# Sink scores behind two scores of their group, and the first expert's weights in halves around v rows

## The chip, the cores and the metric

The kernel runs on one core of a Trainium2 chip. Its time is the device time of one execution in microseconds; a kernel is given by the median of its runs. The engines are TensorE (PE, with its weight loads as PEld), VectorE (DVE), ScalarE (ACT), GpSimd (POOL) and SyncE (SP). POOL and SP also issue the DMA transfers.

## The reference

Attention over a window of 128 keys and four sink keys feeds a mixture of four experts. The sizes are: batch 4, 8 heads, 768 tokens, head dimension 64; 3072 tokens in all for the experts, with model width 512 and hidden width 1024.

```python
scores = scale * np.matmul(q, k.transpose(0, 1, 3, 2))
keep = is_sink | in_window               # 4 sinks, 0 <= i - j < 128
scores = np.where(keep, scores, -1e9)
a = np.exp(scores - max); a = a / (sum(a) + 1e-9)
x = matmul(a, v) as [3072, 512]          # heads side by side
p = domain_probs / (domain_probs.sum(-1, keepdims=True) + 1e-9)
for e in range(4):
    out += p[:, e:e+1] * (relu(x @ w1[e]) @ w2[e])
```

## The kernel before

A batch of attention (`Attention(b)`) is cut into three groups of 256 tokens and four pairs of heads. For each group and pair the steps are: turning of the q and k rows on TensorE (`transposes`, L499, the "flips", into `tr`), a copy of the turned block to `qkT` by ACT or DVE (L222), the window scores (`scores`, L601, `sps`), the exponential on ACT (L626, `aT`), a mask on DVE (L635 in the first batch), the values (`values`, L660 and L667, `od`), the division on DVE (L694, L697, `onat`) and a turn of the result to `xT` (`turn`, L725). In the third and fourth batch the q and k rows are turned by DMA transposes on SP instead (`turn_nat`, L198).

From the second group on, the scores with the four sink keys are a step of their own (`sinks`, L566): four products into one bank, for all four head pairs, and one exponential to `sinkA` (L574). They need the turned q rows of all four pairs of the group and the sink keys `ksd`, which POOL forms for the first batch (L529). The values of the group need `sinkA`.

The expert part (`Mixture`) makes hidden blocks H from `xT` and w1 (L958 and L1035, `hps` and `cps`), gated on DVE with rows that SP loads (`load_gate`, L385), and the output from H and w2 (L1245 for the first batch, L1175 for the others). From the second batch on it uses fewer products, with sums formed on DVE.

A planner written in the kernel sets the order of all engines. It keeps a clock for each engine in the table `t`, with one for the software DMA queue (`t["sw"]`) and one for the hardware DMA queue (`t["hw"]`). It books each step with a fixed cost, and at each turn emits the step that can start soonest by these clocks. Six PSUM banks go round (`pick`, `take`). Within a batch, the steps of keys, sinks and scores come in the order of the list `todo`. Where no step can start within 220 ns of the planner's clock, it puts in a product of zeros (`idle_products`, L481). Loads are issued on POOL in the order of a list, the first of them by the lines that stand ahead of the planner's loop. `lands` books the arrival of a load, and a step that needs it isn't planned ahead of that time. A changed booking or a changed place in `todo` therefore can give another order for all that comes after.

The list for a batch before the change:

```python
for g in range(NG):
    if g == (1 if b == 0 else 0):
        self.todo.append(("keys", b, 0, 0))
    if g:
        self.todo.append(("sinks", b, g, 0))
    self.todo += [("scores", b, hp, g) for hp in range(NHP)]
```

Of the kernel before, what the change touches and what calls it, by code (L numbers as in the profile page):

```python
# [12 lines left out]
BF16 = mybir.dt.bfloat16  # L13
# [3 lines left out]
def kernel(  # L17
# [17 lines left out]
    E, Dm, F = moe_w1.shape  # L35
    Ntok, Dout = out.shape

    P = 128
# [7 lines left out]
    NHP = H // 2  # L46
    NDB = Dm // P
# [23 lines left out]
    t = {"pe": 1200.0, "act": 0.0, "dve": 0.0, "pool": 1280.0, "sp": 800.0, "sw": 6500.0, "hw": 0.0}  # L71
# [81 lines left out]
    landed = {}  # L153
    ROW = {64: 12.8, 128: 22.6, 512: 79.8, 1024: 156.2}

    def lands(key, rows, cols, *deps):
        issued = pool(0, *deps, fixed=880)
        t["sw"] = max(t["sw"], issued + 1500) + rows * ROW[cols] / 16
        landed[key] = t["sw"] + 900
# [8 lines left out]
    wpool = ctx.enter_context(tc.tile_pool(name="wpool", bufs=1))  # L168
# [14 lines left out]
    def load_nat(b, tb):  # L183
        both = sb.tile([P, 2, H, D], BF16, name="qkn", tag="qkn", bufs=NQB)
        for i, src in enumerate((q, k)):
            nc.gpsimd.dma_start(  # L186
                out=both[:, i], in_=src[b, :, tb * P:(tb + 1) * P, :].rearrange("h p d -> p h d"),
            )
            lands(("qk", b, tb), H * P, D, qkn_free[0])
        qkn_free.pop(0)  # L190
        qkn_free.append(1e12)
        nat[b, tb] = both
# [56 lines left out]
    def load_v(b, ts):  # L249
        for tb in ts:  # L250
            nc.gpsimd.dma_start(  # L251
                out=vx[tb][:, :, 0:D],
                in_=v[b, :, tb * P:(tb + 1) * P, :].rearrange("h p d -> p h d"),
            )
            lands(("v", b, tb), H * P, D, values_at[b - 1, min(NG - 1, (tb + 1) // 2)] if b else 0.0)

    w1_sb, w2_sb = {}, {}

    def load_w1(e, parts=1):
        w1_sb[e] = wpool.tile([P, NDB, F], BF16, name=f"w1_{e}", tag=f"w1_{e}")  # L260
        n = F // parts
        for i in range(parts):
            nc.gpsimd.dma_start(
                out=w1_sb[e][:, :, i * n:(i + 1) * n],
                in_=moe_w1[e][:, i * n:(i + 1) * n].rearrange("(db p) f -> p db f", p=P),
            )
            lands(("w1", e, i), Dm, n)
            landed["w1", e] = landed["w1", e, i]

    def load_w2(e):  # L270
        w2_sb[e] = wpool.tile([P, NFB, Dout], BF16, name=f"w2_{e}", tag=f"w2_{e}")
        nc.gpsimd.dma_start(out=w2_sb[e], in_=moe_w2[e].rearrange("(fb p) d -> p fb d", p=P))
        lands(("w2", e), F, Dout)
# [147 lines left out]
    t["sw"] += 500  # L421
    for tb in (2, 3):
        load_nat(0, tb)
    load_v(0, (2, 3))
    load_w1(0, 2)
    t["sw"] += 200
    load_w2(0)

    nc.vector.tensor_copy(out=ident, in_=identf)
# [311 lines left out]
    class Attention:  # L741


        def __init__(self, b):
            self.b = b
            self.flips = [("transposes", b, g, hp) for g in range(NG) for hp in range(NHP)] if b < 2 else []
            self.todo, self.scored, self.valued = [], [], []
            for g in range(NG):
                if g == (1 if b == 0 else 0):
                    self.todo.append(("keys", b, 0, 0))  # L750
                if g:
                    self.todo.append(("sinks", b, g, 0))
                self.todo += [("scores", b, hp, g) for hp in range(NHP)]
            self.total = len(self.todo) + len(self.flips) + (1 if b else 2) * NG * NHP
            self.steps = 0

# [525 lines left out]
    for e in (1, 2):  # L1282
        loads += [(load_w1, e), (load_w2, e)]
# [19 lines left out]
    while mix.more() or att.more():  # L1303
        now = t["pe"]

        if not att.more() and not loaded:
            loaded = 1
            gates_by_row()
            loads += [(load_w1, 3), (load_w2, 3)]
            for tb in range(NQB):  # L1310
                loads.append((load_nat, 1, tb))
                if tb % 2:
                    loads += [(load_v, 1, (tb - 1,)), (load_v, 1, (tb,))]
# [88 lines left out]
```

The softmax here doesn't subtract the row's maximum and nothing guards it: scores larger than these inputs give would overflow.

## Time and profile before

| | |
|---|---|
| median of 5 runs | 379.82 us (379.02 to 381.03) |
| the profiled execution | 379.02 us |
| its span, first to last instruction | 377.3 us |
| TensorE busy | 368.7 us, 3966 products |
| VectorE busy | 270.3 us |
| ScalarE busy | 147.7 us |
| software DMA queue (POOL's) | 17.31 MB, 51.4% of the span of 16 engines |
| hardware DMA queue (SP's and others) | 17.18 MB, 20.8% |

The span is what the profile sees; the time of the execution has a little around it. A busy share is the union of the instructions' times. As products of TensorE overlap in its pipeline, the distance between their starts tells more than their durations. A timeline row gives the start and the length of a series of like instructions in microseconds, the engine, the line and the operation, what is written and read, the shape and the count, and in brackets the idle time ahead of the series with what ended it.

### The profile page before, as it was taken

The page shows a single profiled execution, that of the slowest core. Times are in us where ns is not written, and L with a number is a line of the kernel's source. Part 1 is how long each engine was busy: PE and PEld are TensorE (multiplying, and loading weights), DVE is VectorE, ACT ScalarE, POOL GpSimd, SP SyncE. Part 2 cuts the span into 40 slices and gives each one's busy share as a digit, 9 for nine tenths or more (in the row PEclk, how much of TensorE's full clock was granted, in tenths as well). Part 3 has the DMA queues.
Part 4 walks back from the last instruction along what each step waited for, and adds up shares of the span by engine and source line. Part 5 has one row for each costly group of instructions (what it writes and reads, how often), then busy time and mean ns, then how long its engine had stood idle before and what let it go on. Part 6 is the DMA issues. An engine that isn't in the chain of part 4 may idle for free.

```text
span 377.3 us, 9471 instructions
## 1 busy us (share of the span) xinstructions
PE 368.7 (98%) x3966; PEld 299.6 (79%) x3966; DVE 270.3 (72%) x610; ACT 147.7 (39%) x386; POOL 71.1 (19%) x91
## 2 busy tenths in 40 slices
PE   7999999999999999999998999999999999999995
PEld 3676767566667788888887888889999999999984
DVE  5665987765346997785697499489589496795780
ACT  4856434766455255436415446452112011111110
POOL 8945114702812091010200000000000000000000
PEclk9999999999999999999999999999999999999999
DMA  9999999951999999234394421122021111210101
GB/s 165 176 173 201 210 210 175 155 49 7 144 197 162 198 134 128 71 43 59 70 179 103 57 57 30 30 80 63 0 85 30 55 33 28 71 30 2 57 3 56
DMA packets 110807, 35.61 MB, mean 94 GB/s; under 512 B 94260, under 2 KB 106132, under 8 KB 110764
## 3 DMA queue, kind: packets, MB, share of 16 engines
q0 software_dynamic: 77520, 17.31, 51.4%
q1 hardware_dynamic: 32188, 17.18, 20.8%
q8 instruction: 31, 0.51, 0.6%
q10 hardware_dynamic: 1056, 0.52, 0.5%
q14 instruction: 12, 0.10, 0.1%
HBM read 40.45 MB, written 6.34 MB: 124 GB/s over the span
## 4 chain that ended last, share of the span: by engine, by line
PE 89%; DVE 5%; ACT 2%; DMA 2%; issue 1%; ACTq 0%; DVEq 0%
PE hps L958 28%; PE acc L1175 28%; PE acc L1245 11%; PE cps L1035 11%; PE sps L601 4%; PE od L667 3%; DMA kraw<-in_k_dram 1%; DVE H L982 1%; PE tr L499 1%; ACT onat L706 1%; PE od L660 1%; DMA gates<-gate_rows 1%; DVE H L1054 1%; PE acc L481 1%; PE sinks L566 1%
## 5 line engine op out<-in xcount | busy, mean ns | idle before, releaser
L958 PE MATMUL hps<-xT,w 128*128 128x256 bf16 x1056 | 131.7, 273 | 0.4 <-ACT aT L626 0.2
L958 PEld LDWEIGHTS <-w 128*128 128x128 bf16 x1056 | 99.3, 98 | 14.7 <-issue 2.3
L1175 PEld LDWEIGHTS <-H 128*128 128x128 bf16 x720 | 67.9, 98 | 11.2 <-issue 3.7
L626 ACT ACTIVATE aT<-sps 128x512 bf16<-128x512 f32 (+1 forms) x96 | 47.9, 572 | 34.2 <-PE sps L601 34.2
L982 DVE SCALAR_TENSOR_TENSOR H<-hps,gates 128x512 bf16<-128x512 f32 x84 | 57.3, 686 | 4.7 <-PE hps L958 3.6
L1175 PE MATMUL acc<-w,H 128*128 128x256 bf16 x432 | 56.4, 273 | 0.4 <-ACT acc L1199 0.4
L706 ACT ACTIVATE onat<-od,R 128x64 bf16<-128x64 f32 x144 | 33.2, 323 | 44.5 <-DVE R L694 44.4
L1245 PE MATMUL acc<-w,H 128*128 128x512 bf16 x192 | 45.4, 379 | 0.0
L251 POOL DMA_DIRECT2D vx<-in_v_dram x24 | 21.3, 896 | 80.9 <-PE od L667 70.9
L1175 PE MATMUL acc<-wf,H 128*128 128x256 bf16 x288 | 35.4, 273 | 0.8 <-ACT osb L1208 0.8
L1208 ACT COPY osb<-acc 128x256 f32<-128x256 f32 x36 | 13.5, 374 | 54.9 <-PE acc L1175 54.4
L620 DVE TENSOR_TENSOR aT<-aT,mask 128x1024 bf16<-128x1024 bf16 (+1 forms) x36 | 22.9, 641 | 14.0 <-ACT aT L626 13.9
L1245 PEld LDWEIGHTS <-H 128*128 128x128 bf16 x192 | 18.0, 98 | 18.1 <-issue 0.8
L1035 PEld LDWEIGHTS <-w 128*128 128x128 bf16 x480 | 30.6, 98 | 1.7 <-issue 0.8
L1054 DVE SCALAR_TENSOR_TENSOR H<-cps,gates 128x512 bf16<-128x512 f32 x45 | 30.7, 683 | 0.1
L1175 PEld LDWEIGHTS <-S 128*128 128x128 bf16 x288 | 27.7, 98 | 3.5 <-issue 0.3
L971 ACT ACTIVATE H<-hps 128x512 bf16<-128x512 f32 x35 | 21.1, 605 | 22.3 <-PE hps L958 22.3
L1063 ACT COPY cps<-cps 128x512 f32<-128x512 f32 x15 | 8.7, 582 | 44.1 <-PE cps L1035 44.1
L1035 PEld LDWEIGHTS <-vf 128*128 128x128 bf16 x360 | 22.5, 98 | 0.7 <-issue 0.2
L186 POOL DMA_DIRECT2D qkn<-in_k_dram x22 | 20.1, 913 | 9.8 <-DMA w<-in_moe_w_dram 8.5
L186 POOL DMA_DIRECT2D qkn<-in_q_dram x22 | 20.0, 908 | 8.9 <-DMA w<-in_moe_w_dram 3.9
L1257 DVE SCALAR_TENSOR_TENSOR osb<-acc,scale_t,osb 128x512 f32<-128x512 f32 x18 | 13.5, 749 | 9.4 <-PE acc L1245 9.3
(96 smaller groups left out, 435.8 us busy)
## 6 DMA issues: line engine op xcount, KB each, us to landing
w<-in_moe_w_dram POOLq DMA_DIRECT2D x7, 1024.0 KB, 19.3
out_dram<-osb SPq DMA_DIRECT2D x24, 256.0 KB
gates<-gate_rows SPq DMA_DIRECT2D x36, 128.0 KB
vx<-in_v_dram POOLq DMA_DIRECT2D x24, 128.0 KB, 6.4
qkn<-in_q_dram POOLq DMA_DIRECT2D x22, 128.0 KB, 7.3
qkn<-in_k_dram POOLq DMA_DIRECT2D x22, 128.0 KB, 7.3
w<-in_moe_w_dram POOLq DMA_DIRECT2D x2, 512.0 KB, 7.8
kraw<-in_k_dram ACTq DMA_DIRECT2D x2, 256.0 KB
```

Of the source, the lines that this page charges most:

```text
L186: nc.gpsimd.dma_start(out=both[:, i], in_=src[b, :, tb * P:(tb + 1) * P, :].rearrange("h p d -> p h d"),)
L251: nc.gpsimd.dma_start(out=vx[tb][:, :, 0:D], in_=v[b, :, tb * P:(tb + 1) * P, :].rearrange("h p d -> p h d"),)
L620: nc.vector.tensor_mul(a, a, m[:, None, :].to_broadcast([P, 2, w]))
L626: nc.scalar.activation(out=a[:, ph], in_=sps[ph][:, 0:w], func=AF.Exp, scale=scale)
L706: nc.scalar.mul(o[:, qi, hp, ph * D:(ph + 1) * D], od[:, qi, ph, 0:D], R[:, qi, ph])
L958: nc.tensor.matmul(h[:, i].rearrange("p (q n) -> p q n", q=2), lhsT=w1_sb[e][:, db, fb * P:(fb + 1) * P], rhs=xT[b, g][:, :, db], start=(i ...
L971: nc.scalar.activation(out=dst, in_=h, func=AF.Relu)
L982: nc.vector.scalar_tensor_tensor(out=dst, in0=h, scalar=0.0, in1=gate, op0=ALU.max, op1=ALU.mult,)
L1035: nc.tensor.matmul(y[:, f], lhsT=A[:, d, f * P:(f + 1) * P], rhs=T[:, d], start=(m in ("P1", "P5") and f == 0 and d == 0), stop=(d == 1), ...
L1054: nc.vector.scalar_tensor_tensor(out=dst, in0=src, scalar=0.0, in1=gate, op0=ALU.max, op1=ALU.mult)
L1175: nc.tensor.matmul(x, lhsT=self.operand(b, g, e, m)[:, f], rhs=forms[e][m][:, f], start=(k == 0 and f == 0 and m in ("P1", "P5")), stop=(k ...
L1245: nc.tensor.matmul(op, lhsT=H[:, fb // QF, fb % QF, s], rhs=w2_sb[e][:, fb, :], start=(fb == 0), stop=(fb == NFB - 1),)
```

## The change

It has two parts. The sinks of the first batch now stand in `todo` behind the first two scores of their group, instead of ahead of all four (`insert(2 - NHP, ...)`, that is, two from the end); in the other batches their place stays the same. And of the two halves of expert 0's w1 the first is now issued ahead of the v rows of the blocks 2 and 3 and the second behind them; before, both stood behind. `load_w1` gets a list of parts for that. The booking of the software queue behind the second half grows from 200 to 700.

```diff
-    def load_w1(e, parts=1):
-        w1_sb[e] = wpool.tile([P, NDB, F], BF16, name=f"w1_{e}", tag=f"w1_{e}")
+    def load_w1(e, parts=1, which=None):
+        if e not in w1_sb:
+            w1_sb[e] = wpool.tile([P, NDB, F], BF16, name=f"w1_{e}", tag=f"w1_{e}")
         n = F // parts
-        for i in range(parts):
+        for i in which or range(parts):
             nc.gpsimd.dma_start(
                 out=w1_sb[e][:, :, i * n:(i + 1) * n],
                 in_=moe_w1[e][:, i * n:(i + 1) * n].rearrange("(db p) f -> p db f", p=P),
             )
             lands(("w1", e, i), Dm, n)
-            landed["w1", e] = landed["w1", e, i]
+            if i == parts - 1:
+                landed["w1", e] = landed["w1", e, i]
...
     for tb in (2, 3):
         load_nat(0, tb)
+    load_w1(0, 2, [0])
     load_v(0, (2, 3))
-    load_w1(0, 2)
-    t["sw"] += 200
+    load_w1(0, 2, [1])
+    t["sw"] += 700
     load_w2(0)
...
                 if g == (1 if b == 0 else 0):
                     self.todo.append(("keys", b, 0, 0))
+                self.todo += [("scores", b, hp, g) for hp in range(NHP)]
                 if g:
-                    self.todo.append(("sinks", b, g, 0))
-                self.todo += [("scores", b, hp, g) for hp in range(NHP)]
+                    self.todo.insert(2 - NHP if b == 0 else -NHP, ("sinks", b, g, 0))
```

## The prediction

> **What bounds the kernel now.** I read first the busy shares and the 40 slices of the page, then the chain that ended last, then the timeline of each engine over the first 36 us, then the waits of TensorE and of the DMA queue.
>
> ```profile
> span 377.3 us, 9471 instructions
> ...
> PE 368.7 (98%) x3966; PEld 299.6 (79%) x3966; DVE 270.3 (72%) x610; ACT 147.7 (39%) x386; POOL 71.1 (19%) x91
> ...
> PEclk9999999999999999999999999999999999999999
> ...
> PE 89%; DVE 5%; ACT 2%; DMA 2%; issue 1%; ACTq 0%; DVEq 0%
> ```
>
> TensorE is in use for 98% of the span and carries 89% of the chain. Busy time hides small gaps, so I took the start-to-start distances of its 3,963 products. Without a wait they are fixed: 109 ns for 256 columns, 216 for 512, 56 for 128, 29 for a values product, and about 95 ns more on entering and again on leaving a run of scores or sinks. With these distances the stream is 363.1 us long, and 9.1 us are waits: 2.2 before 16.3 us, 1.4 from there to 42 us, 1.2 from 65 to 75 us, none from 75 to 180 us, 1.7 from 200 to 245 us, and 1.2 in the last 15 us, where the last chunk's operands are formed. The other 5 us are before the first product and after the last. So the change can save only products, runs of scores, or waits of TensorE. It touches this stretch first:
>
> ```profile
> 14.59 0.83 PE L499 MATMUL tr<-ident,qkn 128*128 128x128 bf16 x12
> 15.26 1.15 PE L481 MATMUL acc<-lent 128*128 128x256 bf16 x9
> 16.33 0.35 PE L566 MATMUL sinks<-qkT,ksd 128*32 128x256 bf16 x4
> 16.61 0.95 PE L601 MATMUL sps<-qkT 64*128 64x128 bf16 x18
> 17.50 0.39 PE L481 MATMUL acc<-lent 128*128 128x256 bf16 x2
> 17.90 1.05 PE L958 MATMUL hps<-xT,w 128*128 128x256 bf16 x8
> ```
>
> The sinks wait until all four head pairs of the group are turned; nine filling products (L481) stand in that gap, two more ahead of the first product of expert 0. What they wait for:
>
> ```profile
> 14.74 1.63 ACT L222 COPY qkT<-tr 128x512 bf16<-128x512 bf16 x3 [0.68 <-PE tr L499]
> ...
> 15.38 0.41 DVE L222 COPY qkT<-tr 128x512 bf16<-128x512 bf16 x1
> ...
> 17.90 0.77 PEld L958 LDWEIGHTS <-w 128*128 128x128 bf16 x8 [0.29 <-DMA w<-in_moe_w_dram]
> ```
>
> The last copy ends at 16.37. The weight load at 17.90 was released by the first half of w1.
>
> **The change part by part.** The changed kernel's instruction order is a new plan from here to the end, with the same computing instructions; only filling products differ, 27 for 34. Two turning copies go from DVE to ACT and two xT copies the other way: the same count, on engines that wait.
>
> *Filling products:* 9 and 2 go, 4 come after the last scores of the group: -7 x 0.109 = -0.77 us.
>
> *Runs of scores and sinks:* I count 47 before and 49 after, as the sinks and four heads no longer stand in one run: 2 x 0.19 = +0.38 us. The sum of the fixed distances is thus -0.39 us.
>
> *DMA issues:* on POOL's queue the first half of w1 is issued at 9.16 instead of 10.89, ahead of the two v loads, which issue 0.75 us later each; the second half, w2 and the key products of POOL (13.27) keep their places and times. The loads land in order of issue. The last k row before them and the half itself:
>
> ```profile
> L186 POOL DMA_DIRECT2D qkn<-in_k_dram x1: 923/923/923, 8.3 to 8.3; - x1
> DMA to landing us min/median/max: 4.6/4.6/4.6
> ...
> L263 POOL DMA_DIRECT2D w<-in_moe_w_dram x1: 823/823/823, 10.9 to 10.9; - x1
> DMA to landing us min/median/max: 7.0/7.0/7.0
> ```
>
> The k row lands at 12.9; the v rows then landed at 13.7 and 14.6, the half at 17.9, 3.3 us after them. In the new order: half 12.9 + 3.3 = 16.2, v rows 17.1 and 17.9, second half 20.35 as before (same bytes ahead of it). The Trainium skill (DMA: Bandwidth & Descriptors, Anatomy of one DMA) fits one such DMA as 2.0 us plus bytes over 436 GB/s: for this half (1 MB read as float32) that is 4.4 us, and the half would be there at 13.6. The trace has 7.0 us behind loads still in flight, so the margin is not 3 us but 0.4. I take the trace; by the rule the sum is the same, since either is before the use at 16.6, but only by the rule would there be room for more.
>
> *The walk through the new order* (durations from the rows above and their neighbours; ACT's exponentials leave every 0.50 us, DVE's masks take 0.33, an H step 0.60, reciprocal and multiply 0.55): scores of head pair 0 at 15.35 and of pair 1 at 15.85; sinks at 16.33, not earlier, since they still need the fourth copy; first product of expert 0 at 16.6. Scores of pair 2 at 17.5; the second product needs the bank of the third exponential (17.95): 18.0. The sink exponential is now behind four score exponentials on ACT (16.37 + 4 x 0.50 + 0.39 = 18.75): everything queued behind it there moves with it, and the values, which need it, start at 18.9, two pairs together; the v rows at 17.9 are hidden under that by 1.0 us. Scores of pair 3 at 19.7, four filling products to 20.5, then the first turn: its onat is behind an H step, a mask, a reciprocal and a multiply on DVE, done at 20.75, a wait of 0.25. Third product 20.85 (second half landed 20.35), the rest of the group to 23.5, first product of the second group at 23.75. Before, this last mark stood at 23.93 after the same work. So of 0.58 us (0.77 less one more run) only about 0.2 us is kept: DVE and ACT set this stretch, and the waits that the filling products covered come back under other names.
>
> *Third group of the first batch:* before, the sinks and scores wait here too (0.17, 0.25 and 0.05 us at 33.0 to 33.9). The new order puts a whole output product (1.73 us) between the turning and the scores, and another behind the sinks: these waits go, -0.46; one more run, +0.19. What is late next is nothing until 65 us, as TensorE then has only products of landed experts.
>
> *Second batch's rows:* they land as before, since the total of bytes ahead of them is unchanged (blocks 2 and 3 at 70.9). In the new order their turning stands 1.45 us of stream earlier (at 62.5 us of it instead of 63.9; before, it ran at 72.8). It comes to about 70.8: a wait of 0.1 to 0.3. Of the waits there now (1.2 us, four of them) some go as more work stands between copy and use. I take the two as even.
>
> *Later moves:* on POOL the v rows 1 and 2 of the third batch go behind twelve row loads. They landed at 95 to 99 and would land by about 115; first values of that batch are at about 128: hidden by 13 us. The rows go 1.7 us earlier. On SP all six transposes of the fourth batch now stand together behind one output store, instead of five. I take nothing.
>
> *The removed filling products and the clock:* in the trace, products ran at half rate (427 ns for 512 columns) until about 6.8 us and never again; the wait of 0.67 us at 8.3 changed nothing. The skill (TensorE: Matmul & The Clock Gate, HAM oscillation) speaks against taking fillers out: idle gaps over about 3.4 us bring the clock back to half. By the row the cost is 0; by the rule, if it struck, at least 3.4 us at half rate, 1.7 us lost, 381.1 in all. The longest gap of the walk is 0.3 us, so I take 0.
>
> *Sum:* -0.2 (second group) - 0.27 (third) + 0 = about -0.45 us; for plans that differ I allow waits of 0.7 us either way, as most of the 22 waits after 16 us are 0.05 to 0.4 us each. The profiled execution took 379.02 us (span 377.3 and 1.7 around it), so 378.6; the median of the five runs is 0.8 above it, so 379.4.
>
> **The rivals.**
> *The new plan also loses waits that the old one had:* the gates of the fourth batch (below) and the product waits at 212 and 242 us (0.33 each), with half of those at 65 to 75. For it: the stretch at 75 to 180 shows that a plan with none is possible. Against: the same engines serve the same work. 0.6 + 0.6 + 0.3 more: 377.9.
>
> *The fourth batch's gates become the bound, and it is slower.*
>
> ```profile
> 189.58 7.01 SPq L198 DMA_TRANSPOSE qkT<-qkn  x3
> 196.69 0.53 SPq L1205 DMA_DIRECT2D out_dram<-osb  x1
> 197.31 1.29 SPq L684 DMA_TRANSPOSE xT<-onat  x1
> 198.70 1.98 SPq L385 DMA_DIRECT2D gates<-gate_rows  x4
> ```
>
> and on TensorE's timeline:
>
> ```profile
> 203.77 0.34 PE L601 MATMUL sps<-qkT 64*128 64x256 bf16 x4 [0.98 <-ACT onat L706]
> ```
>
> The gates stand behind six transposes on SP, which start after the last scores of the third batch, and land at 201.9, 18.3 us after those. DVE waits for them at the next H step, and TensorE at 203.77 for what DVE held up (1.05 us). In the new order TensorE reaches the hidden block of that step 0.44 us sooner (16.6 us of stream after the scores, not 17.0), and a later product needs the very bank that the step empties: arrival 18.3, bank free at 18.3 + 0.7 + 0.1, a wait of 0.8 in place of 1.05. That is no loss. It decides the sign only if what DVE holds (a T step, a sum and a second H step, 1.5 us) falls on TensorE as well, 2.7 us instead of 1.05: 379.4 + 1.7 = 381.1.
>
> *The change does nothing:* the half of w1 lands earlier but the sinks' copies and DVE set the stretch. This is two thirds of my walk; 379.8.
>
> **How the numbers follow.** A measurement of this kernel tells about 0.3% (1.14 us) from no change. My forecast (379.4, with its own range 378.7 to 380.5) and "nothing" together 0.56: within 0.3%. The plan that loses waits 0.24: faster. The gates, or a like wait where DVE or ACT is behind in the new order, 0.20: slower. The range takes in 377.9 and 381.1 and the run to run spread of the five (2.0 us): 377.8 to 381.6.
>
> **What would show it.** Right: no filling products between 15.3 and 16.3; expert 0's first product at 16.6 without a DMA wait; v rows landed before 18.8; sink exponential near 18.4; first product of the second group near 23.75; no wait at 33; stream 362.7. Wrong: weights later than 16.7 or a wait at the first values (the landing order is not the issue order); products at double distance near 16 us (the clock); the gain at 24 us near 0.6 (DVE was not the limit); a wait of over 2 us near 200.

## The result and the profile after

The changed kernel takes 378.57 us (median of 29 runs, 377.25 to 379.37); the kernel before took 379.95 us beside it (50 runs, 378.56 to 381.31). The ratio is 0.9965, with a 95% interval of 0.9957 to 0.9973: 1.3 us faster, just above what a measurement of this kernel can tell from no change. The forecast was 379.4 us and "within 0.3%". The time lies inside the range, but the gain is about three times the forecast one, and nearer to the 377.9 of the rival in which the new plan also loses waits of the old one, to which the forecast gave a chance of 0.24.

The two profiled executions do not show this difference. The one of before (379.02 us) is 0.9 us faster than its median, the one of after (379.16 us) is 0.6 us slower than its own. The spans are therefore equal, and the gain has to be read stretch by stretch. The page of after (its line numbers are three higher than those of before):

```profile
span 377.5 us, 9455 instructions
...
PE 368.4 (98%) x3959; PEld 298.8 (79%) x3959; DVE 270.1 (72%) x610; ACT 148.5 (39%) x386; POOL 71.0 (19%) x91
...
PEclk9999999999999999999999999999999999999999
...
PE 88%; DVE 6%; DMA 2%; ACT 2%; issue 1%; ACTq 0%; DVEq 0%
```

TensorE is still in use for 98% of the span. The waits of TensorE, by its start-to-start distances (a distance counts as a wait by what it has above the usual one of its kind, if that is over 0.02 us; the last row holds all the rest):

| stretch, us | before | after | difference |
|---|---|---|---|
| 7 to 24 | 2.34 | 3.96 | +1.62 |
| 24 to 42 (third group) | 1.09 | 0.56 | -0.53 |
| 42 to 90 | 0.82 | 0.88 | +0.06 |
| 90 to 180 | 0.00 | 0.08 | +0.08 |
| 180 to 260 | 1.73 | 0.86 | -0.87 |
| 260 to the end | 1.23 | 1.23 | 0 |
| all the rest | 365.04 | 364.81 | -0.23 |

The last column adds up to +0.13, by which the distance from the first start to the last is longer in after. So the profile of after holds gains of 1.6 us, and losses of 1.8 us that hide them. The largest loss, 1.27 us, is one row in TensorE's timeline (start, length, what runs, and the wait ahead of it):

```profile
14.37 0.39 PE L502 MATMUL tr<-ident,qkn 128*128 128x128 bf16 x4
15.86 0.29 PE L728 MATMUL tx<-ident,onat 128*128 128x128 bf16 x2 [1.10 <-DVE onat L700]
...
17.81 0.27 PE L569 MATMUL sinks<-qkT,ksd 128*32 128x256 bf16 x1 [0.20 <-ACT qkT L222]
18.01 1.05 PE L961 MATMUL hps<-xT,w 128*128 128x256 bf16 x8
```

A turn of the first group waits for a division on DVE; from start to start this is 1.27 us above the fixed distance. All that follows is late by about that much: the first product of expert 0 starts at 18.01 and not at the 16.6 of the forecast. DVE's timeline in the same stretch, and then POOL's:

```profile
13.34 1.91 DVE L453 TENSOR_SCALAR mask<-lent 128x384 bf16<-128x384 bf16 x1
15.17 0.17 DVE L697 RECIPROCAL R<-od 128x4 f32<-128x4 f32 x1
15.38 0.42 DVE L700 TENSOR_TENSOR onat<-od,R 128x256 bf16<-128x256 f32 x1
```

```profile
13.31 0.73 POOL L532 TENSOR_TENSOR ksd<-qkT,half 128x8 bf16<-128x8 bf16 x4
13.95 1.18 POOL L547 TENSOR_TENSOR vsd<-vsf,sel 128x520 bf16<-128x520 f32 x1
```

The mask step, which forms one of the two masks, takes 1.91 us here. It starts 0.03 us behind POOL's key products and ends at 15.25, 0.1 us behind the last of POOL's five products. In the profile of before the same step starts ahead of them. DVE's timeline of before, then POOL's:

```profile
13.23 0.25 DVE L450 TENSOR_SCALAR mask<-lent 128x384 bf16<-128x384 bf16 x1
13.39 0.18 DVE L694 RECIPROCAL R<-od 128x4 f32<-128x4 f32 x1
13.60 0.42 DVE L697 TENSOR_TENSOR onat<-od,R 128x256 bf16<-128x256 f32 x1
13.94 1.31 DVE L450 TENSOR_SCALAR mask<-lent 128x512 bf16<-128x512 bf16 x1
```

```profile
13.27 0.75 POOL L529 TENSOR_TENSOR ksd<-qkT,half 128x8 bf16<-128x8 bf16 x4
13.98 1.12 POOL L544 TENSOR_TENSOR vsd<-vsf,sel 128x520 bf16<-128x520 f32 x1
```

There it takes 0.25 us, and the division runs behind it at once. Only the second mask takes 1.31 us, when no division waits behind it. The Trainium skill (SBUF — State Buffer, Who interferes with whom) says that DVE in its two-port modes and GpSimd share a pair of ports as a lock: the one that issues first holds it for the whole instruction, and the other is blocked. The rows agree as to which one is blocked: 0.25 us ahead of POOL, 1.91 us behind it. They show more than the page's sentence: the step stood still for the whole row of five POOL instructions, and not for one. That a port is what blocks it is the page's reading; no view names it.

In the third group the new plan did as forecast. TensorE's timeline of after has no wait between the turning and the scores, where before had 0.17 and 0.25 us:

```profile
32.91 1.06 PE L502 MATMUL tr<-ident,qkn 128*128 128x128 bf16 x16
33.81 1.89 PE L1248 MATMUL acc<-w,H 128*128 128x512 bf16 x8
35.63 0.56 PE L604 MATMUL sps<-qkT 64*128 64x128 bf16 x10
```

The first half of w1 was issued on POOL's queue at 9.2 us and landed 7.1 us later, at 16.3:

```profile
L264 POOL DMA_DIRECT2D w<-in_moe_w_dram x1: 784/784/784, 9.2 to 9.2; - x1
...
DMA to landing us min/median/max: 7.1/7.1/7.1
```

At the fourth batch's gates, SP's timeline of after and the product that waits on TensorE:

```profile
184.66 0.34 SPq L1190 DMA_DIRECT2D out_dram<-osb  x1
185.62 12.22 SPq L198 DMA_TRANSPOSE qkT<-qkn  x6
197.93 0.53 SPq L1208 DMA_DIRECT2D out_dram<-osb  x1
198.55 1.29 SPq L687 DMA_TRANSPOSE xT<-onat  x1
199.93 1.98 SPq L387 DMA_DIRECT2D gates<-gate_rows  x4
```

```profile
203.95 1.03 PE L961 MATMUL hps<-xT,w 128*128 128x256 bf16 x8 [0.52 <-DVE H L985]
```

The gates are issued at 199.93 us, 15.2 us behind the last scores of the third batch (184.77), as in before (15.25). TensorE waits 0.69 us from start to start (forecast 0.8, before 1.05), and at a product of the hidden block instead of at a score.

The greater part of the 0.87 us of waits that went between 180 and 260 us is not at the gates. In before, two output products wait for ACT to copy out the bank that they write to; from start to start these waits are 0.33 us each:

```profile
212.57 0.60 PE L1175 MATMUL acc<-wf,H 128*128 128x256 bf16 x4 [0.17 <-ACT osb L1208]
...
242.00 0.60 PE L1175 MATMUL acc<-wf,H 128*128 128x256 bf16 x4 [0.17 <-ACT osb L1208]
```

In after, other work stands in these places, at the second of them a hidden block, and the wait is gone:

```profile
241.77 0.61 PE L1038 MATMUL cps<-xT,vf 128*128 128x128 bf16 x8
242.22 1.04 PE L961 MATMUL hps<-xT,w 128*128 128x256 bf16 x8
```

This holds for every profile on record. The five kernels with the old order of the sinks have both product waits (0.33 us each) and both waits of the third group (0.17 and 0.20 us); the five with the new order have none of the four. They have one new wait of 0.13 us near 233 us.

### The profile page after: what moved, and what is told of

Same layout as the page of the kernel before. It is cut to its first block, busy times and chain, and to the rows that moved or that the text cites. A ratio compares the mean times of both kernels' runs of the same rounds, so it can differ in the third digit from the quotient of the medians.

```text
span 377.5 us, 9455 instructions
## 1 busy us (share of the span) xinstructions
PE 368.4 (98%) x3959; PEld 298.8 (79%) x3959; DVE 270.1 (72%) x610; ACT 148.5 (39%) x386; POOL 71.0 (19%) x91
## 4 chain that ended last, share of the span: by engine, by line
PE 88%; DVE 6%; DMA 2%; ACT 2%; issue 1%; ACTq 0%; DVEq 0%
PE acc L1178 29%; PE hps L961 28%; PE cps L1038 12%; PE acc L1248 11%; PE sps L604 3%; PE od L670 2%; DVE H L985 2%; DMA kraw<-in_k_dram 2%; PE tr L502 1%; ACT aT L629 1%; PE od L663 1%; DMA gates<-gate_rows 1%; DVE onat L700 1%; PE tx L728 1%; DVE H L1057 0%
## 5 line engine op out<-in xcount | busy, mean ns | idle before, releaser
L1038 PEld LDWEIGHTS <-vf 128*128 128x128 bf16 x360 | 22.6, 98 | 0.6
```

The lines of the kernel that those rows point to most:

```text
L1038: nc.tensor.matmul(y[:, f], lhsT=A[:, d, f * P:(f + 1) * P], rhs=T[:, d], start=(m in ("P1", "P5") and f == 0 and d == 0), stop=(d == 1), ...
```

## The experiments

Three theories were open. By the first, the gain is at the gates of the fourth batch, whose wait would then be longer in most executions of before than in its profile. By the second, the gain is at the opening, in the stretch that the change touches. The third is about the loss: the mask step decides the opening, by its start against POOL's. Two sets were run; each was timed beside the kernel before on its own chip (380.56 us, median of 31 runs, for the first four kernels, 380.37 us, 23 runs, for the others).

**The sinks' place alone.** The lines of `todo` as in the change, the loads as before:

```diff
-                if g:
-                    self.todo.append(("sinks", b, g, 0))
                 self.todo += [("scores", b, hp, g) for hp in range(NHP)]
+                if g:
+                    self.todo.insert(2 - NHP if b == 0 else -NHP, ("sinks", b, g, 0))
```

> Only the new place of the sinks; both halves of w1 stay behind the v rows. The order also has seven filling products fewer. Stage theory (the gain is fillers less two runs of scores, 0.37 us, the third group's waits, 0.43, and waits of the later plan, 0.5): 1.0 us or more faster than before, ratio near 0.997, with a wait for the first half of w1 of up to 0.5 us near 17 us. Rival (the gain needs the early weights): expert 0's first product waits to 17.9 us and the gain is under 0.4 us.

Measured: 379.01 us (12 runs), ratio 0.9956 [0.9941, 0.9972]. This is the whole gain of the change within the intervals. In its profile the largest distance from start to start near 204 us is 0.42 us (before 1.25), and the first product of the second group starts at 24.35 us (before 23.93), so there is no gain at the opening in this kernel either. There the first half of w1 landed only at 18.72 us (17.85 in before), and the first product of expert 0 waited 0.55 us for it, started at 18.76, and yet the gain came. The rival of the expectation, by which the gain needs the early weights, is thus refuted. What the early half adds to the sinks' new place is nothing that these runs can tell.

**The early half of w1 alone.** The load lines as in the change, the sinks ahead of their group as before:

```diff
+    load_w1(0, 2, [0])
     load_v(0, (2, 3))
-    load_w1(0, 2)
-    t["sw"] += 200
+    load_w1(0, 2, [1])
+    t["sw"] += 700
```

> Only the order of the loads and the booking of 700; the sinks stay ahead of their four scores. Two filling products fewer than before, runs of scores as before. Stage theory: the sinks still wait for the fourth copy, so 0.2 us of fillers and what the later plan brings, 0 to 0.5 us: ratio 0.998 to 1.000. Rival (the weights are what was late): near the whole gain, 0.9965.

Measured: 381.94 us (12 runs), ratio 1.0046 [1.0023, 1.0069], slower. The profiled execution is the slowest of these (384.53 us) and shows what such an execution has. TensorE's timeline near 204 us, and below it a table of busy time by stretch (length, busy time of PE, PEld, DVE, ACT and POOL), in which the granted TensorE clock stands behind the last engine:

```profile
207.70 0.34 PE L604 MATMUL sps<-qkT 64*128 64x256 bf16 x4 [2.11 <-ACT onat L709]
207.97 2.03 PE L1178 MATMUL acc<-w,H 128*128 128x256 bf16 x12
209.80 1.06 PE L1178 MATMUL acc<-wf,S 128*128 128x256 bf16 x4
```

```profile
7.40:10.80 3.40, 1.86 (x21) 0.91 (x20) 1.99 (x4) 1.94 (x6) 3.40 (x5) 1.00 2.16 137
10.80:14.20 3.40, 3.40 (x33) 1.55 (x30) 1.29 (x4) 2.88 (x9) 3.40 (x9) 0.50 1.51 150
205.30:208.70 3.40, 1.29 (x14) 0.88 (x13) 2.80 (x7) 1.51 (x6) 0.00 (x0) 1.00 0.33 95
208.70:212.10 3.40, 3.40 (x20) 1.98 (x19) 1.26 (x4) 1.38 (x4) 0.00 (x0) 0.51 0.00 0
```

Behind the wait the clock is at half for 3.4 us, and four products take 1.06 us where they otherwise take 0.60. So one late gate costs twice: 2.2 us of wait, and about 1.6 us more by products at half rate. The opening of this execution has such a spell too, from 10.8 to 14.2 us, behind two waits of TensorE near 8.8 and 9.6 us; against the same kernel with six gate buffers (below), which has no such spell, it cost 1.0 us. What DVE waited for near 204 us is the gates themselves:

```profile
205.90 0.69 DVE L985 SCALAR_TENSOR_TENSOR H<-hps,gates 128x512 bf16<-128x512 f32 x1 [1.98 <-DMA gates<-gate_rows]
```

**The masks early, in the changed kernel and in the one before.** The two mask steps are issued on DVE behind its first cast near 5 us, eight microseconds ahead of POOL's key and value products; the planner's bookings stay, and TensorE's order is the same:

```diff
     def make_mask(i):
         def run(engine):
-            x = (mask0, mask1)[i]
-            nc.vector.tensor_scalar(out=x, in0=low[i], scalar1=1 / LOW, scalar2=1.0, op0=ALU.mult, op1=ALU.add)
             dve(4 * P)
...
+                if (half, i) == (0, 0):
+                    for x, y in zip((mask0, mask1), low):
+                        nc.vector.tensor_scalar(out=x, in0=y, scalar1=1 / LOW, scalar2=1.0, op0=ALU.mult, op1=ALU.add)
```

> The changed kernel, with the two mask steps of VectorE issued right behind its first cast, near 5 us, instead of near 13 us beside GpSimd's key and value products; all bookings and TensorE's order are the same. Race theory (in the changed kernel's profile a mask step of 0.25 us took 1.9[...], and the turn at 15.9 waited 1.27 us for it; this goes one way or the other from run to run): the masks take 0.25 and 0.34 us, no wait over 0.2 us near 15.9, the median 0.3 to 0.8 us below the changed kernel, ratio to before about 0.995, and less scatter. Rival (something else held the step): the median stays at 0.9965 and the wait moves to another step.

> The kernel before with the same move of the two mask steps. If the race costs the kernel before as often as the changed one, it falls by the same 0.3 to 0.8 us (ratio about 0.9985) and the change's own gain stays 0.35%. If it costs only the changed kernel (in the profile of before the masks took 0.25 and 1.3 us and TensorE did not wait), this one stays within 0.1% of before, and the change's gain without the race is more than 0.35%. If it costs only the kernel before, this one is as fast as the changed kernel.

Measured: the changed kernel 378.36 us (8 runs), ratio to before 0.9946 [0.9928, 0.9964]; the kernel before 380.04 us (12 runs), 0.9991 [0.997, 1.0012], no difference. The mask steps took 0.66 and 0.27 us there. The interval of the changed kernel overlaps that of the change alone (0.9957 to 0.9973), so a gain by early masks is not shown. In its profile the wait at 15.86 us is gone, and the next one comes up. TensorE's weight loads in that kernel:

```profile
17.12 0.77 PEld L962 LDWEIGHTS <-w 128*128 128x128 bf16 x8 [0.81 <-DMA w<-in_moe_w_dram]
```

The half of w1 landed at 17.08 us in this execution, and the weight load stood for 0.81 us until then. As TensorE's order is the same as in the changed kernel, the starts of the two profiles can be laid side by side: 1.1 us are won at 15.86 us, 0.9 are lost again by 22.1 us to late weights, and 0.7 are won at the gates, which were issued 14.4 us behind the last scores and not 15.2. The profiled execution of before with early masks (383.14 us, again the slowest of its kernel) shows the other loss once more: the gates were issued 16.2 us behind the last scores, and TensorE waited 2.8 us. TensorE's timeline:

```profile
206.31 0.34 PE L602 MATMUL sps<-qkT 64*128 64x256 bf16 x4 [2.75 <-ACT onat L707]
206.58 1.83 PE L1176 MATMUL acc<-w,H 128*128 128x256 bf16 x12
208.21 1.06 PE L1176 MATMUL acc<-wf,S 128*128 128x256 bf16 x4
```

**Six gate buffers instead of five, in four kernels.** With a sixth buffer one more block of gates is loaded ahead of the transposes. DP is cut from 72 to 68 to make room; TensorE's order is the same as with five. A run of DP at 68 with five buffers was not made.

```diff
-    NGATE = 5
+    NGATE = 6
...
-    DP = 72
+    DP = 68
```

> The kernel before with six gate buffers instead of five, so that every gate load is issued one unit sooner; the rows of v are padded to 68 instead of 72 to make room; TensorE's order is unchanged. Gates theory (most of the change's gain is the wait for the fourth batch's gates near 204 us, which is 1.0 us in the profile of before, 2.2 and 2.8 us in two other profiles of that order, and there followed by products at half rate): no wait over 0.3 us between 195 and 212 us, no half rate, and 1.0 to 2.5 us faster than before, ratio 0.9935 to 0.9975. Opening theory (the gain comes from the fillers and the third group's waits, before 42 us): at most 0.5 us faster, ratio 0.9985 or more.

> The changed kernel with six gate buffers and the same padding, TensorE's order unchanged. Gates theory: its wait near 204 us is only 0.7 us and less in some runs, so it gains 0.2 to 0.7 us, and the distance to the kernel before with six buffers shrinks to 0.3 to 0.9 us. Opening theory: both gain the same, and the distance stays at 1.3 us.

> Only the order of the loads changed (sinks ahead of the scores as before), with six gate buffers. With five, the profile showed 2.2 us of waiting for the gates and 3.4 us at half rate after it. Gates theory: this goes, and it falls by 2 us or more, from a ratio of 1.0046 to 0.995 to 0.999, near the kernel before with six buffers. If the early weights are themselves bad for the opening, it stays above 1.000.

> The changed kernel with the mask steps early and six gate buffers: the version that both theories make the fastest. Race and gates theory: 0.3 us or more below the changed kernel with six buffers alone, ratio to before 0.992 to 0.9945, no wait over 0.5 us between 10 and 360 us. Rival (the masks were never on the path except in a rare run): equal to six buffers alone within 0.1%.

Measured:

| kernel | median, us (runs) | ratio to before | with five buffers |
|---|---|---|---|
| before, six | 379.27 (12) | 0.9966 [0.9955, 0.9978] | 1 |
| changed, six | 378.39 (6) | 0.9937 [0.9918, 0.9955] | 0.9965 |
| w1 alone, six | 380.12 (12) | 0.9988 [0.9975, 1.0001] | 1.0046 |
| changed, masks early, six | 377.72 (6) | 0.9936 [0.9914, 0.9957] | 0.9946 |

In all four profiles the largest distance from start to start near 204 us is 0.33 us. The same score as in the kernel before, on TensorE's timeline of before with six buffers, starts without a wait that the row would name:

```profile
202.39 0.60 PE L1175 MATMUL acc<-w,H 128*128 128x256 bf16 x4
203.03 0.34 PE L601 MATMUL sps<-qkT 64*128 64x256 bf16 x4
203.31 1.48 PE L1175 MATMUL acc<-w,H 128*128 128x256 bf16 x12
```

What follows for the kernel before and the changed one. The edit took 1.1 us off the median of before (0.22 to 0.45%), more than the opening theory's 0.5 us, so that theory fell as stated. In both pairs of profiles the starts of TensorE with five and with six buffers are within 0.2 us of each other from 8 us to the gates, and 0.7 us apart from there to the end (0.9 us are won at the gates in before, 0.7 in the changed kernel). So the new DP by itself moved nothing that these profiles show. The gates are not the whole difference between before and after, as the sixth buffer helps both. With six buffers 0.88 us are left between the medians (ratio 0.9937 / 0.9966 = 0.9971, give or take 0.0022), with five 1.33 by that kernel's ratio. The gates' share in the gain is the distance between these two, and the intervals leave it between nothing and nearly all. For the rest the profiles show what no gate touches: the four waits that every profile of the old order has and none of the new, 1.0 us together, less the new one of 0.13.

What follows for w1 alone. The sixth buffer takes it back from +0.46% to -0.12%, but it still stands 0.85 us above the kernel before with six buffers (ratio 0.9988 / 0.9966 = 1.0022, give or take 0.0017). So the gates are a part of its slowness, and the opening is another: in the profiles with six buffers its first product of the second group starts at 26.15 us, in before with six at 24.00. In both profiles of w1 alone, with five buffers and with six, a turn near 26 us waits 0.9 us from start to start for a division on DVE, which before does not. TensorE's timeline with six:

```profile
26.02 0.28 PE L728 MATMUL tx<-ident,onat 128*128 128x128 bf16 x2 [0.74 <-DVE onat L700]
```

With six buffers the mask step is seen again. DVE's timeline of the changed kernel with six buffers:

```profile
13.32 1.93 DVE L453 TENSOR_SCALAR mask<-lent 128x384 bf16<-128x384 bf16 x1
```

That execution took 378.40 us. Of the six runs of this kernel four took 378.38 to 378.57 us and two 376.97 and 377.31, and the distance of 1.2 us between the two sets fits the 1.27 us of the mask step. This is an inference; no profile of one of the short runs exists, and the 29 runs with five buffers show no such gap. Early masks then bring nothing in the interval (0.9936 for 0.9937), since in the profile of that kernel both halves of w1 came late. Its weight loads:

```profile
17.34 0.77 PEld L962 LDWEIGHTS <-w 128*128 128x128 bf16 x8 [1.32 <-DMA w<-in_moe_w_dram]
...
22.65 0.77 PEld L962 LDWEIGHTS <-w 128*128 128x128 bf16 x8 [1.13 <-DMA w<-in_moe_w_dram]
```

The changed kernel with six gate buffers beats both kernels, with early masks or without.

## Why the prediction was right or wrong

**The fixed stream: right in its counts.** Seven filling products fewer and 49 runs of scores for 47 are what the profile has. The stream without the waits became 0.23 us shorter (forecast 0.39); it holds the distances under 0.02 us too.

**The loads: right in the profile of after, but the margin was no margin.** Forecast 16.2 us for the first half, 17.1 and 17.9 for the v rows, 20.35 for the second half; measured 16.33, 17.19, 18.03 and 20.57. The 0.4 us between landing and use at 16.6 came from one execution. Where the masks did not hold the opening, the half landed at 17.08 and 17.30 us and the second at 21.87 and 22.61, and the products behind them started 0.2 and 0.7 us late at the first half and 0.6 and 1.1 us at the second. The order of landing held; its time scatters by 1 to 2 us.

**The walk to 23.75 us: not seen.** The first product of the second group starts at 25.06 us in the profile of after. Without the 1.27 us of the mask step it would be 23.79, so the walk by itself agrees with the profile but for this step. It took the mask step at its length in the profile of before (0.25 us) and did not ask what made it so short. No profile of a changed kernel reached 23.93, the mark of before: 25.06 with the mask step behind POOL (also with six buffers), 24.84 and 25.57 with late weights. The gain of 0.2 us at the opening is therefore shown nowhere.

**The third group: right.** Waits of 0.46 us were to go; the stretch lost 0.53.

**The second batch's rows: right.** Taken as even; the stretch from 42 to 90 us changed by 0.06.

**"On SP all six transposes of the fourth batch now stand together ... I take nothing": right for the profile, not for other executions.** In the profiles the gates came as late behind the last scores as before (15.2 us), and the forecast wait (0.8 for 1.05) measured 0.69. What the step left out is what varies. With an output store between the first and second transpose, the time from the first issue of a transpose to the last was 11.1 us in before and 11.8 and 12.1 in the two kernels that waited long; with the store ahead of all six it was 10.6 in after, 10.2 with the sinks' place alone and 9.9 with early masks. With six buffers it was 10.3 and 10.6 in the old order, 9.7 and 9.2 in the new. And the wait falls elsewhere: in before on a score, through ACT's `onat` and DVE's `R`, which is queued behind the gated step; in after on a product whose bank that step empties, with 0.4 us less wait at the same lateness of the gates. Two kernels with the old order of the sinks had waits of 2.2 and 2.8 us there; none with the new order had over 0.7. These are single profiled executions, so they show what can happen and not how often.

**The slower rival: a wait of its size is real, by another way and on the other side.** It needed about 2.7 us at the gates, by work that DVE holds. Waits of 2.2 and 2.8 us came in two kernels with the old order of the sinks, with half rate on top, and there the gates themselves were later: issued 16.2 us behind the last scores.

**"+ 0" for all that follows the third group: the step that failed.** The sum was -0.2 - 0.27 + 0, with 0.7 us either way for "plans that differ", and against the rival that loses waits it said that "the same engines serve the same work". The stretch from 180 to 260 us lost 0.87 us: 0.36 at the gates, 0.33 at the product of 212 us and 0.33 at that of 242, less 0.13 at 233 and 0.04 at 208. The rival had named the gates and these two products, and only its half of the waits at 65 to 75 us stayed. The edit does not aim at these places. It changed the planner's order there as a side effect, so this part of the gain is luck: no step of the forecast led to it. The two product waits are gone in all five profiles with the new order.

**From the profile to the median: taken over without a reason.** The forecast put the 0.8 us by which the median of before lies above its profile on the changed kernel as well. But that 0.8 is not a constant of the chip. The sixth gate buffer alone took 1.1 us off the median of before, while the profiled executions differ by 0.7. The changed kernel's profile lies above its median, with the mask step in it. Without that step it would be at about 377.9, 1.1 us below the profile of before and 0.7 below its own median; the medians differ by 1.4. This agreement is not proof, since how often each kernel loses the mask step, and how long the gates are late in each, was not counted.

**The clock: right for the change, but no fixed guard.** The waits of after, up to 1.27 us, brought no half rate. The Trainium skill's limit (TensorE: Matmul & The Clock Gate, HAM oscillation) is gaps over about 3.4 us; in these runs gaps of 2.4 and 3.0 us from start to start were enough, and in the opening of w1 alone two waits of 1.06 and 0.48 us within 3.4 us, so here the measurement decides. Where half rate struck it lasted 3.4 us and cost 1.6 us near 209 us, as the prediction's sum for that case had it (1.7).

What stays open: the share of the gates in the gain; how often each kernel loses the mask step; and the time with DP at 68 by itself. The sinks' place with six buffers, and early masks with six buffers in the kernel before, were not tried.

## What to carry to other kernels

An edit that changes a planner's order changes waits far from the lines that it touches. A forecast that puts these at nothing should name the waits that stand there now, and ask for each what would stand in its place. Before a stage's length is taken from one profile, ask which of its steps start within a tenth of a microsecond of another engine's step that can block them, or end within a microsecond of a landing: these fall differently in other executions, and their cost belongs in the range. A median that lies well above its profiled execution is a finding by itself: some wait is usually longer than the profile shows, and the longest chain of transfers on one queue is the first place to look. Where small loads stand behind such a chain, one more buffer, so that a block of them is issued ahead of it, was here worth about as much as the whole change.

## What the runs showed of the hardware

A mask step of 128x384 elements on DVE took 0.25 us when it started 0.04 us ahead of POOL's products, and 1.91 us when it started 0.03 us behind them. When it started at 14.09 us, within the last of these products (w1 alone with six buffers), it took 1.15 us, and when it started at 15.38, behind them all (w1 alone), 0.25 us again. The profiles whose first scores (waiting on the first rows) started by 8.33 us had the step ahead of POOL's products, those at 8.41 and 8.43 us (the changed kernel) just behind their start. The changed loads are issued only at 9.2 us, so this shift need not come from the change, and before may lose the step in some executions too; no profile shows that.

TensorE's clock fell to half three times behind its waits in these profiles, for 3.4 us each time. In the 3.4 us ahead TensorE had been busy for 1.29 us (w1 alone near 207 us, and before with early masks) and for 1.86 us (the opening of w1 alone). In w1 alone with six buffers waits of 2.04 and 0.44 us in the opening brought no half rate; from 7.7 to 11.1 us TensorE was busy for 1.92 us. So the length of a gap alone does not tell.

The first half of w1, issued at the same place of the queue, landed between 16.3 and 17.3 us in the changed kernel with and without early masks and sixth buffer, and the second half between 20.6 and 22.6.
